# Five two-input operations in place of one strided reduction, for phi's maximum and its sum of weights

## The chip, the cores and the metric

The kernel runs on one core of one Trainium2 chip. The metric is the device time of one execution in microseconds (us), lower is better. The median of the runs of the kernel before is what a change is held against; the profile is of one single execution, whose own time stands beside its span below.

## The reference, cut to what matters

An attention with a small memory feeds two feed-forward blocks. Only the first lines concern the change: `phi` becomes softmax weights `a` over its 32 columns, and `a` gathers keys and values into a memory of 32 rows for each of 4 x 8 heads.

```python
a = phi - np.max(phi, axis=2, keepdims=True)      # phi: 4 x 8 x 576 x 32, the maximum over the 576 tokens
a = np.exp(a)
a = a / (np.sum(a, axis=2, keepdims=True) + 1e-09)
k_m = np.einsum('bhsm,bhsd->bhmd', a, k)
v_m = np.einsum('bhsm,bhsd->bhmd', a, v)
scores = scale * np.matmul(q, k_m.transpose(0, 1, 3, 2))
attn = softmax(scores)                             # over the 32 columns
x = np.matmul(attn, v_m)                           # then as 2304 rows of 512
h = x @ w_in;  g = h / (1 + np.exp(-h));  x = g @ w_out
out = ((x @ w_a) * (x @ w_b)) @ w_out2
```

All arrays come in as 64-bit floats, of which the kernel makes 32-bit values, or pairs of a high and a low part that are multiplied as three products.

## The kernel before, in words

Each batch b goes through `weights(b)`, `memory(b)`, and for its two groups of four heads `turn_q`, `scores` and `softmax`. The feed-forward block starts in between (`unit`: `emit_h` at L279, `emit_y` at L303), as soon as a batch's attention is there, and the second block (`emit_ab`, `emit_out`) follows when all is done.

`weights(b)` is the function that changes. `load_phi` (L416) has put phi of one batch into the tile `ph`: 96 partitions, each with 8 heads x 6 tokens x 32 columns, so a partition holds six tokens of each head. L450 reduces the six tokens on VectorE (DVE) to a maximum per head and column, in `mxa`. Its input is a view with the tokens innermost, so neighbouring elements of the read lie 32 words apart. TensorE transposes `mxa` (L455), L459 reduces over the 96 partitions, and L463 and L465 spread the result back to all partitions. L472 subtracts it, on GpSimd (POOL) for batches 0 to 2 and on DVE for batch 3, and L475 takes the exponential. Batch 0 is done in two halves of four heads (`SPLIT_W`), so L450 runs five times. For batch 3 alone (`SUMS`), L478 reduces the six tokens again, as a sum, and a matmul with a column of ones (L489) finishes it; the other batches get their sums from a matmul with ones in `memory` (L506).

The weights of the feed-forward blocks come in by `load_w` (L93) or, later, `convert` (L157): a transfer into `st`, issued by SyncE (SP), then a run of dependent DVE operations (L107, L110, L113, L117, L124) that builds the 32-bit value, with ScalarE (ACT) and POOL taking a part. `st` has three buffers, so a further load waits until an earlier one has been read for the last time.

The order on each engine is not that of the program text alone. The calls from L593 on give the order in which the work is written down; the tile framework then plans the order of each engine's instructions with its own estimates of what each costs (`schedule_with_timeline_sim=True`, L830), unless a line pins it (`tc.keep_in_program_order`). On the chip each engine runs its list in that fixed order.

Of the kernel before, what the change touches and what calls it, by code (L numbers as in the profile page):

```python
# [14 lines left out]
ALU = mybir.AluOpType  # L15
AX = mybir.AxisListType
# [4 lines left out]
def attn_moe_moe2_kernel(  # L21
# [24 lines left out]
    nc = tc.nc  # L46
# [334 lines left out]
    JP = S // P  # L381
# [8 lines left out]
    def warm_up(w, n):  # L390

        if n:
            jk = ff["y"].tile([128, HALF], F32, tag="yp", name="jk")
            for _ in range(n):
                nc.tensor.matmul(jk[:P, :P], w[:, :P], ones, start=True, stop=True)
# [16 lines left out]
    def heads(b):  # L412

        return [slice(0, 4), slice(4, 8)] if b in SPLIT_W else [slice(0, 8)]
# [17 lines left out]
    def load_q(b, hg):  # L432
# [7 lines left out]
                nc.sync.dma_start(out=qq[r], in_=src[o])  # L440
        st[b]["qq", hg] = qq

    def weights(b, sub=nc.vector):

        e = st[b]["ph"]
        for hs in heads(b):
            nh = hs.stop - hs.start
            n = nh // 4
            mxa = p_s.tile([P, nh, NM], F32, tag="mxa", bufs=2, name="mxa")
            nc.vector.tensor_reduce(  # L450
                out=mxa, in_=e[:, hs].rearrange("p h c m -> p h m c"), op=ALU.max, axis=AX.X
            )
            mxt = ps_t.tile([128, n, P], F32, tag="t", name="mxt")
            for x in range(n):
                nc.tensor.transpose(  # L455
                    mxt[:, x], mxa[:, 4 * x : 4 * x + 4].rearrange("p h m -> p (h m)"), ident[:P, :P]
                )
            mx = p_s.tile([128, n], F32, tag="mx", bufs=2, name="mx")
            nc.vector.tensor_reduce(out=mx, in_=mxt, op=ALU.max, axis=AX.X)  # L459

            dg = p_s.tile([128, n, 128], F32, tag="mxa", bufs=2, name="dg")
            for x in range(n):
                nc.scalar.activation(out=dg[:, x], in_=ident, func=AF.Copy, scale=mx[:, x : x + 1])  # L463
            bc = ps_t.tile([P, nh, NM], F32, tag="t", name="bc")
            nc.tensor.matmul(bc.rearrange("p h m -> p (h m)"), ones, dg.rearrange("p x n -> p (x n)"))  # L465
            if b == 0:
                warm_up(dg[:, 0], WARM[1 + hs.start // 4])
            if sub is nc.gpsimd:
                mxb = p_s.tile([P, nh, NM], F32, tag="mxa", bufs=2, name="mxb")
                nc.scalar.activation(out=mxb, in_=bc, func=AF.Copy)  # L470
                bc = mxb
            sub.tensor_tensor(  # L472
                out=e[:, hs], in0=e[:, hs], in1=bc.unsqueeze(2).to_broadcast([P, nh, JP, NM]), op=ALU.subtract
            )
            nc.scalar.activation(out=e[:, hs], in_=e[:, hs], func=AF.Exp)  # L475
            if b in SUMS:
                es = p_s.tile([P, nh, NM], F32, tag="mxa", bufs=2, name="es")
                nc.vector.tensor_reduce(  # L478
                    out=es, in_=e[:, hs].rearrange("p h c m -> p h m c"), op=ALU.add, axis=AX.X
                )  # L480
                if "sm" not in st[b]:
                    st[b]["sm"] = ps_t.tile([128, 2], F32, tag="t", name="sm")
                for x in range(n):
                    g = hs.start // 4 + x

                    for y in range(2):
                        r = slice(64 * y, 64 * y + 64)
                        hd = 4 * x + (2 * y + 2 * b) % 4
                        nc.tensor.matmul(  # L489
                            st[b]["sm"][r, g : g + 1], es[:, hd : hd + 2].rearrange("p h m -> p (h m)"), ones[:P, :1]  # L490
                        )
# [106 lines left out]
    load_phi(1)  # L598
    load_phi(2)
    weights(0, nc.gpsimd)  # L600
    load_kv(0, 1)
    memory(0)
# [4 lines left out]
    scores(0, 0)  # L607
    load_kv(1, 0)
    weights(1, nc.gpsimd)
    load_wo(0, 0, (nc.vector, nc.vector, nc.vector))  # L610
    turn_q(0, 1)
# [10 lines left out]
    memory(1)  # L622
    load_wo(0, 2, (nc.gpsimd, nc.gpsimd, nc.vector))
    weights(2, nc.gpsimd)
    turn_q(1, 0)
    unit(0, 0, 0, cs=(0, 1))
# [208 lines left out]
```

## Time and profile before

| | us |
|---|---|
| median of 3 runs | 893.93 |
| lowest and highest of them | 891.17, 895.27 |
| the profiled execution, its own time | 895.07 |
| its span, first to last instruction | 893.3 |
| TensorE (PE) busy in the span | 847.2 |
| DVE busy | 536.1 |
| ACT busy | 406.3 |
| POOL busy | 162.5 |

The span lies 1.77 us under the execution's own time. Busy times are sums over the whole span; the first 80 us, in which phi, the keys and the first weights come in, look quite unlike the rest. A row of instruction groups gives line, engine, operation, output and inputs with their shapes, the count, then busy time in us and the mean of one in ns, then the idle time ahead of it. In a timeline a row is start, duration, engine, line.

### The profile page before, as it was taken

How to read it: one execution, taken by the hardware profiler on the slowest of the kernel's cores; microseconds unless marked ns; L12 is line 12 of the kernel's file. 1: busy time of each engine (PE TensorE's matmuls, PEld its weight loads, DVE VectorE, ACT ScalarE, POOL GpSimd, SP SyncE). 2: the span in 40 equal slices, each digit the busy share in tenths (PEclk: the TensorE clock that was granted, in tenths of full speed). 3: DMA queues.
4: the chain of work that ended last, by engine and by line, in shares of the span. 5: the costliest groups of instructions: out<-in, count | busy, mean ns of one | idle time of the engine just before them, and what ended most of it. 6: DMA issues, size and time to landing. Idle time of an engine off the chain costs nothing.

```text
span 893.3 us, 14183 instructions
## 1 busy us (share of the span) xinstructions
PE 847.2 (95%) x5654; PEld 799.8 (90%) x5654; DVE 536.1 (60%) x980; ACT 406.3 (45%) x819; POOL 162.5 (18%) x160
## 2 busy tenths in 40 slices
PE   5458899999999999999999999999999999999998
PEld 4347889999999999999999999999999999999997
DVE  3699688887777677766755544636445552233313
ACT  2347666686566566555444332333333332122211
POOL 3454003422210111121222111111111110000000
PEclk7557999999999999999999999999999999999999
DMA  9998410265752554364764434424343321110012
GB/s 213 244 202 211 108 27 26 83 152 109 156 122 45 116 127 99 85 143 105 160 134 98 92 84 95 95 59 93 85 95 72 83 48 24 36 36 20 24 30 71
DMA packets 49939, 87.16 MB, mean 98 GB/s; under 512 B 4561, under 2 KB 26065, under 8 KB 49873
## 3 DMA queue, kind: packets, MB, share of 16 engines
q1 hardware_dynamic: 33456, 56.50, 24.3%
q0 software_dynamic: 16128, 29.37, 18.7%
q8 instruction: 44, 0.72, 0.3%
q10 hardware_dynamic: 288, 0.39, 0.2%
q14 instruction: 23, 0.18, 0.1%
HBM read 52.17 MB, written 4.72 MB: 64 GB/s over the span
## 4 chain that ended last, share of the span: by engine, by line
PE 80%; DMA 7%; DVE 6%; issue 3%; ACT 2%; SPq 1%; POOL 1%; POOLq 0%; DVEq 0%; ACTq 0%
PE ab L742 32%; PE yp L312 19%; PE op L763 17%; PE hp L288 9%; DMA st<-in_moe_w_in_dram 3%; DMA t_w<-e_w 1%; PE mp L268 1%; PE mp L256 1%; PE sc L556 1%; DMA kv<-in_v_dram 1%; DVE t L113 1%; DMA wo_1l<-t_wo 1%; SPq L427 1%; DVE qT L539 1%; SPq L98 0%
## 5 line engine op out<-in xcount | busy, mean ns | idle before, releaser
L747 DVE TENSOR_TENSOR asb<-ab,asb 128x384 f32<-128x384 f32 x72 | 40.1, 557 | 198.8 <-PE ab L742 196.0
L746 ACT ACTIVATE asb<-ab 128x384 f32<-128x384 f32 x72 | 35.4, 491 | 148.8 <-PE ab L742 148.8
L79 ACT ACTIVATE ph<-asb 128x384 fp32r<-128x384 f32 x72 | 37.6, 522 | 118.9 <-DVE asb L747 118.8
L298 ACT ACTIVATE g<-hp 128x288 f32<-128x288 f32 x128 | 52.3, 411 | 79.9 <-PE hp L288 71.7
L300 DVE TENSOR_TENSOR gl<-g,gh 128x288 fp32r<-128x288 f32 x128 | 62.2, 488 | 38.5 <-ACT gh L299 38.1
L187 POOL DMA_DIRECT2D t_w<-e_w x36 | 31.8, 884 | 145.8 <-DVE e_w L183 130.3
L318 DVE TENSOR_TENSOR y<-yp,y 128x288 f32<-128x288 f32 x104 | 47.3, 456 | 18.4 <-PE yp L312 17.9
L299 ACT ACTIVATE gh<-g 128x288 fp32r<-128x288 f32 x128 | 56.4, 444 | 3.6 <-PE yp L312 0.3
L75 DVE TENSOR_TENSOR pl<-asb,ph 128x384 fp32r<-128x384 f32 x72 | 39.9, 554 | 20.7 <-ACT ph L79 20.7
L79 ACT ACTIVATE yh<-y 128x768 fp32r<-128x768 f32 (+1 forms) x48 | 29.5, 676 | 25.9 <-PE ab L742 25.9
L312 PE MATMUL yp<-gh,wo_1l 128*128 128x288 f32 x128 | 37.8, 296 | 1.5 <-DMA wo_1l<-t_wo 1.5
L312 PE MATMUL yp<-gh,wo_0h 128*128 128x288 f32 x128 | 38.4, 300 | 0.1
L312 PE MATMUL yp<-gh,wo_2h 128*128 128x288 f32 x128 | 38.2, 299 | 0.0
L312 PE MATMUL yp<-gl,wo_3h 128*128 128x288 f32 x128 | 37.8, 297 | 0.0
L312 PE MATMUL yp<-gl,wo_2h 128*128 128x288 f32 x128 | 37.8, 295 | 0.0
L312 PE MATMUL yp<-gl,wo_0h 128*128 128x288 f32 x128 | 37.8, 295 | 0.0
L312 PE MATMUL yp<-gh,wo_2l 128*128 128x288 f32 x128 | 37.7, 295 | 0.0
L312 PE MATMUL yp<-gh,wo_3h 128*128 128x288 f32 x128 | 37.7, 295 | 0.0
L312 PE MATMUL yp<-gl,wo_1h 128*128 128x288 f32 x128 | 37.7, 296 | 0.0
L312 PE MATMUL yp<-gh,wo_1h 128*128 128x288 f32 x128 | 37.7, 294 | 0.0
L312 PE MATMUL yp<-gh,wo_0l 128*128 128x288 f32 x128 | 37.7, 294 | 0.0
L312 PE MATMUL yp<-gh,wo_3l 128*128 128x288 f32 x128 | 37.6, 294 | 0.0
(416 smaller groups left out, 2861.4 us busy)
## 6 DMA issues: line engine op xcount, KB each, us to landing
t_w<-e_w POOLq DMA_DIRECT2D x36, 256.0 KB, 4.9
st_wi<-in_moe_w_in_dram SPq DMA_DIRECT2D x12, 512.0 KB, 4.3
st_wo<-in_moe_w_out_dram SPq DMA_DIRECT2D x12, 512.0 KB, 3.7
st_w<-in_moe_w_a_dram SPq DMA_DIRECT2D x12, 512.0 KB, 3.9
st_w<-in_moe_w_b_dram SPq DMA_DIRECT2D x12, 512.0 KB, 4.0
st_w<-in_moe_w_out_dram SPq DMA_DIRECT2D x12, 512.0 KB, 3.8
kv<-in_k_dram SPq DMA_DIRECT2D x8, 576.0 KB, 11.7
kv<-in_v_dram SPq DMA_DIRECT2D x8, 576.0 KB, 14.3
```

What stands on the lines that cost most here:

```text
L75: eng_lo.tensor_tensor(out=lo, in0=src, in1=hi.bitcast(F32), op=ALU.subtract)
L79: nc.scalar.activation(out=out, in_=in_, func=AF.Copy)
L288: nc.tensor.matmul(hp, a[:, cs], x[b][:, kc, ts], start=(n == 0), stop=(n == 5))
L298: nc.scalar.activation(out=g32, in_=hp, func=AF.Silu)
L299: nc.scalar.activation(out=gh, in_=g32, func=AF.Copy)
L300: nc.vector.tensor_tensor(out=gl, in0=g32, in1=gh.bitcast(F32), op=ALU.subtract)
L312: nc.tensor.matmul(yp, a[:, os], x, start=(n == 0), stop=(n == 3 * len(cs) - 1))
L318: nc.vector.tensor_tensor(out=ys, in0=yp, in1=ys, op=ALU.add)
L742: nc.tensor.matmul(abp, a[:, ks], yy[:, kc], start=(n == 0), stop=(n == 11))
L746: nc.scalar.activation(out=asb, in_=ps[0], func=AF.Copy)
L747: nc.vector.tensor_tensor(out=asb, in0=ps[1], in1=asb, op=ALU.mult)
L763: ins = nc.tensor.matmul(o_t[x], a[:, cols], w, start=(c == 0 and n == 0), stop=(c == 3 and n == 2))
```

## The change

L450 and L478 each become a call of a new helper, `over_tokens`. It makes the result by five two-input operations on DVE: the first takes tokens 0 and 1, each further one takes the result so far and the next token. In each, 32 columns of a head lie side by side in all three operands. The output tile, its shape and everything else stay. The sum's additions keep the order of the tokens.

```diff
+    def over_tokens(out, x, op):
+        for c in range(1, JP):
+            nc.vector.tensor_tensor(out=out, in0=x[:, :, 0] if c == 1 else out, in1=x[:, :, c], op=op)
+
     def weights(b, sub=nc.vector):
...
-            nc.vector.tensor_reduce(
-                out=mxa, in_=e[:, hs].rearrange("p h c m -> p h m c"), op=ALU.max, axis=AX.X
-            )
+            over_tokens(mxa, e[:, hs], ALU.max)
...
-                nc.vector.tensor_reduce(
-                    out=es, in_=e[:, hs].rearrange("p h c m -> p h m c"), op=ALU.add, axis=AX.X
-                )
+                over_tokens(es, e[:, hs], ALU.add)
```

## Rows read from the trace of the kernel before

**Rows 1.** Stretches: length, busy PE, PEld, DVE, ACT, POOL; clock, DMA share, GB/s
```profile
20.00:40.00 20.00, 6.38 (x104) 4.96 (x105) 14.05 (x25) 8.54 (x21) 9.20 (x7) 0.50 1.07 249
40.00:60.00 20.00, 15.13 (x212) 12.02 (x214) 17.48 (x25) 7.17 (x14) 8.12 (x5) 0.59 0.89 195
60.00:80.00 20.00, 12.79 (x51) 8.84 (x44) 19.84 (x33) 11.59 (x27) 14.20 (x8) 0.59 1.08 234
80.00:100.00 20.00, 19.95 (x269) 18.91 (x267) 17.76 (x25) 15.69 (x29) 2.14 (x1) 0.98 0.51 140
```

**Rows 2.** The chain that ended last: start, us, what
```profile
13.05 15.27 DMA st<-in_moe_w_in_dram
...
50.37 2.70 DVE mxa L450
...
78.05 3.63 PE sc L556 x8
...
119.26 2.65 issue
```

**Rows 3.** DVE, groups of instructions by shape, first 130 us
```profile
L113 DVE SCALAR_TENSOR_TENSOR t<-e,t 128x512 uint32<-128x512 uint32 x8 | 9.9, 1232 | 0.2
...
L450 DVE TENSOR_REDUCE mxa<-ph 96x256 f32<-96x1536 f32 x3 | 8.4, 2797 | 1.7 <-DMA ph<-in_phi_dram 1.7
L300 DVE TENSOR_TENSOR gl<-g,gh 128x288 fp32r<-128x288 f32 x16 | 6.9, 447 | 0.6 <-ACT gh L299 0.6
...
L450 DVE TENSOR_REDUCE mxa<-ph 96x128 f32<-96x768 f32 x2 | 2.9, 1471 | 6.5 <-DMA ph<-in_phi_dram 4.5 <-ACT mxb L470 2.0
L478 DVE TENSOR_REDUCE es<-ph 96x256 f32<-96x1536 f32 x1 | 2.9, 2870 | 0.0
...
L127 DVE TENSOR_TENSOR t<-t,e 128x512 f32<-128x512 f32 x4 | 2.7, 663 | 0.0
L75 DVE TENSOR_TENSOR vbd_lo<-vt,vbd_hi 64x64 fp32r<-64x64 f32 x12 | 2.6, 215 | 0.2
...
L472 DVE TENSOR_TENSOR ph<-ph,bc 96x1536 f32<-96x1536 f32 x1 | 1.7, 1740 | 0.0
```

**Rows 4.** DVE in order of time, 9 to 25 us
```profile
9.38 1.38 DVE L539 STREAM_TRANSPOSE qT<-qq 128x1152 f32<-128x1152 f32 x1 [3.43 <-DMA qq<-in_q_dram]
...
12.93 1.47 DVE L450 TENSOR_REDUCE mxa<-ph 96x128 f32<-96x768 f32 x1 [2.03 <-ACT mxb L470]
...
19.85 2.77 DVE L450 TENSOR_REDUCE mxa<-ph 96x256 f32<-96x1536 f32 x1 [1.71 <-DMA ph<-in_phi_dram]
22.55 0.41 DVE L110 TENSOR_SCALAR t<-e 128x512 uint32<-128x512 uint32 x1
22.99 0.69 DVE L113 SCALAR_TENSOR_TENSOR t<-e,t 128x512 uint32<-128x512 uint32 x1
```

**Rows 5.** POOL in order of time, 10 to 92 us
```profile
12.59 1.81 POOL L472 TENSOR_TENSOR ph<-ph,mxb 96x768 f32<-96x768 f32 x1 [7.81 <-ACT mxb L470]
17.92 1.89 POOL L472 TENSOR_TENSOR ph<-ph,mxb 96x768 f32<-96x768 f32 x1 [3.52 <-ACT mxb L470]
...
75.76 3.90 POOL L472 TENSOR_TENSOR ph<-ph,mxb 96x1536 f32<-96x1536 f32 x1
87.88 2.14 POOL L572 TENSOR_TENSOR x<-x,mxq 128x1152 f32<-128x1152 f32 x1 [8.23 <-DVE mxq L571]
```

**Rows 6.** DVE in order of time, 74 to 92 us
```profile
78.29 2.84 DVE L450 TENSOR_REDUCE mxa<-ph 96x256 f32<-96x1536 f32 x1
...
88.25 2.32 DVE L75 TENSOR_TENSOR wo_3l<-t,wo_3h 128x512 fp32r<-128x512 f32 x1
```

**Rows 7.** SP, its queue's issues in order of time, 0 to 90 us
```profile
24.94 0.35 SPq L98 DMA_DIRECT2D st<-in_moe_w_out_dram  x1
```

**Rows 8.** Waits of PE, 0 to 84 us: total, times, longest
```profile
PE kvp L506 <- DMA kv<-in_v_dram: 3.6, 1, 3.6
```

**Rows 9.** Waits of PE, 84 to 140 us: total, times, longest
```profile
PE sm L489 <- DVE es L478: 0.4, 1, 0.4
```

## The prediction

> **What bounds the kernel now.** I read the table of stretches first. From 80 us on PE is full: 19.95 of 20 us in the first stretch after it. Before, three things take turns. Between 20 and 40 us PE has 6.38 us of work and the transfers take 1.07 of the DMA engines' time, so loading is the limit. Between 60 and 80 us DVE is busy 19.84 of 20 us, while PE has 12.79 [rows 1]. The reader should see from this that DVE time is worth something only in a stretch of some 30 us, and after it only where PE happens to wait for a single DVE result.
>
> The chain of waits, read next, says where the changed lines lie in that picture [rows 2]. It runs through a transfer (13.05 to 28.3 us), later through DVE, in which batch 2's maximum stands with 2.70 us, and goes over to PE at 78.05 us. Batch 3's sum stands there too: the 2.65 us called issue, from 119.26 to 121.91, are the time in which L478 ran. PE lost less by it: its waits show 0.4 us for `es` [rows 9], since it had other products until then.
>
> **The price of a step.** The groups by shape give it [rows 3]. A two-input operation of 288 columns takes 447 ns and one of 512 takes 663, so a column costs (663 - 447) / 224 = 0.96 ns, and 256 columns cost 447 - 31 = 416 ns. For 128 columns I go up from the row of 64: 215 + 62 = 277 ns. The steps depend on each other. L110 and L113 do too: L113 starts at 22.99, L110 ended at 22.55 + 0.41 [rows 4], a gap of 0.03 us. So five steps of 256 take 5 x 0.416 + 4 x 0.03 = 2.20 us, five of 128 take 1.50.
>
> The reductions take 2.797, 1.471 and 2.870 us [rows 3]. That is 1.82 ns for each of 1536 elements, while the subtraction of L472, which reads the same tile in runs of 32 words, takes 1740 ns for as many, 1.13 ns each [rows 3]. Here is the gain: the view with tokens innermost reads slowly. Per long maximum it is 2.80 - 2.20 = 0.60 us, for the sum 0.67; a short one loses 0.03. In all DVE is relieved of 3 x 0.60 + 0.67 - 2 x 0.03 = 2.4 us out of 536.
>
> No row shows this very step. Its ends: the columns alone, 256 x 0.96 = 0.25 us, so five in 1.23 and a long maximum better by 1.57; and the row of 512, 0.663, so five in 3.44 and worse by 0.64. I take 0.416, as 288 columns is the nearest row in size, and keep both ends.
>
> The Trainium skill, Vector Engine (DVE) Microarchitecture Reference, section 5.2 (Measured stream behaviour on trn2), puts about 75 ns beside 1.04 ns a column for instructions that follow each other in the queue. By that five steps would be an estimate of 1.71 us and the whole sum about -1.5 us. No row here shows it for operations that wait for each other.
>
> **What comes with two inputs.** DVE's operations of two inputs can be held up by POOL; the reductions are not. Batch 3's maximum ran from 78.29 with POOL busy until 75.76 + 3.90 = 79.66 and took 2.84 [rows 5, 6], 0.04 more than the mean. In contrast `wo_3l`, two inputs of 512 columns, began at 88.25 while POOL worked from 87.88 to 90.02; it took 2.32 and ended 0.55 after POOL did [rows 5, 6]. I read it as: a step that meets a running POOL operation waits for its end.
>
> This is also a rule of the Trainium skill (SBUF — State Buffer, section Who interferes with whom): on this chip `tensor_reduce` never contends with GpSimd, while an instruction with two SBUF inputs waits out a GpSimd instruction that reads SBUF. It speaks against the change. By it the memsets at the start, which read nothing, would hold nobody; no row decides that.
>
> **The six places in turn.**
> - Batch 0, first half (about 4.5 us): nothing. The next DVE work but one, `qT`, sits idle 3.43 us for its transfer [rows 4], which covers 0.03 and more.
> - Batch 0, second half: it starts at 12.93, under POOL's subtraction, 12.59 to 14.40 [rows 4, 5]. Held, it ends at 14.40 + 1.50 = 15.90 instead of 14.40. POOL's second subtraction then starts at 17.92 + 1.50 = 19.42 and ends at 21.31. The products on batch 0's weights come later by as much; PE waited 3.6 us for `v` there [rows 8], which hides it.
> - Batch 1, at 19.85: now under that subtraction, held for 1.46, then 0.60 shorter, so what is behind it on DVE, L110 at 22.55 and its successors, is 0.86 late. They release an `st` buffer, and SP's load of 24.94 waits for that [rows 7], with the other loads behind it in SP's queue. I cost this at nothing, because the DMA engines have 1.07 of their time filled there [rows 1]. Without that cover it is +0.86.
> - Batch 2, at 50.37: on the chain, nothing of POOL named beside it: -0.60.
> - Batch 3's maximum, at 78.29: held 1.37, then 2.20, so it ends 0.73 later. The chain has gone over to PE a quarter of a microsecond before. PE's products from 78.05 to the next DVE operand cover it. Without that cover +0.73.
> - Batch 3's sum: 0.67 less for DVE, of which PE gets the 0.40 that it waited [rows 9]. What is late next is the run of gates and results behind it on DVE, and they move up by the same 0.67.
>
> Sum: -0.60 - 0.40 = -1.0 us. Against the profiled execution, 895.07 (span 893.3), that is 894.1; this execution lies 1.1 above the median of 893.93, so for the median I say 892.9. With the ends it goes from -1.57 - 0.40 = -2.0 to 2 x 0.64 + 0.86 + 0.73 = +2.9.
>
> **What can upset this: the order.** The plan of each engine's order is made anew. That it departs from the text can be seen: `qT` of the call after `memory(0)` runs at 9.38, ahead of batch 0's second maximum at 12.93 [rows 4]. Thirty steps in place of six, with other costs in the plan, can move their neighbours.
>
> **Rivals.** A measurement of this kernel can tell about 0.5%, 4.5 us, from no change.
> - A luckier order. DVE lost much to holding: L113 averages 1.232 us over eight, against 0.69 unheld [rows 3, 4], 4.3 us in all. If the new order lets these fall beside POOL's work, the time is -1.0 - 4.3 = -5.3, 888.6. For it: most of this lies where DVE is the limit. Against it: nothing in the change aims at it, and all eight would have to profit.
> - Steps held in the stretch where DVE is the limit. One instruction becomes five, and between two of them a POOL operation can begin. POOL has 14.20 us in 8 operations between 60 and 80 us [rows 1], 1.8 each. If batch 2's maximum is planned in there, or POOL's work beside it, four holds cost 7.1: 7.1 - 1.0 = +6.1, 900.0. The first hold eats the gain; over 0.5% it takes the fourth. For it: the holding is seen. Against: POOL is busy only 8.12 of 20 us between 40 and 60 [rows 1].
> - The read is no faster in steps: the gain goes, 893.9. L472's row is against it. It is no change, as is my forecast.
>
> **How the numbers follow.** The forecast, with the last rival, gets 0.58: the effect is small by every row, and PE's 800 us behind do not change. The luckier order gets 0.24, the held steps 0.18. The forecast's own range is -2.0 to +2.9 with 2 us of scatter, 890 to 898.8. For 8 in 10 I reach into both others: 886.5 to 899.5. Faster by over 0.5% is 0.24, same 0.58, slower 0.18; the time is the likeliest case's, 892.9.
>
> **What would show it.** Each long maximum as five rows of about 0.42 us, 2.2 from first to last; first steps stretched to about 1.8 us where POOL's subtraction runs; PE's wait for `es` gone; the chain's change to PE near 77.5 us instead of 78.05. It is wrong if the order on DVE between 44 and 78 us is another, if the steps take over 0.55 us, or if PE's start of full work moves by more than 2 us either way.

## The result, and the profile after

The changed kernel takes 904.63 us (median of 4 runs, 899.16 to 908.37) against 894.60 for the kernel before in the same session: ratio 1.0114, 95% interval 1.0068 to 1.016. It is slower by over 0.5%; I had forecast 892.9 and given this side 0.18. The profiled execution of the changed kernel is its quickest, 899.16, with a span of 897.4.

Where the lines of before answer to it: the stretches [rows 1], with the two pieces of 2 us that follow a new pause of PE. Columns as there; the third number from the end is the granted clock.

```profile
20.00:40.00 20.00, 7.22 (x91) 5.24 (x86) 12.23 (x25) 8.20 (x20) 9.64 (x7) 0.50 1.07 254
40.00:60.00 20.00, 10.42 (x218) 8.65 (x216) 18.42 (x34) 7.67 (x13) 7.70 (x6) 0.84 1.00 232
60.00:80.00 20.00, 11.97 (x38) 8.77 (x39) 19.88 (x33) 10.61 (x26) 14.52 (x8) 0.67 0.92 212
80.00:100.00 20.00, 18.65 (x258) 17.49 (x257) 15.79 (x22) 15.52 (x27) 2.13 (x1) 0.97 0.33 99
...
140.00:160.00 20.00, 15.61 (x102) 14.75 (x101) 17.14 (x33) 12.13 (x20) 5.89 (x5) 0.91 0.09 27
...
156.00:158.00 2.00, 2.00 (x12) 2.00 (x11) 2.00 (x5) 0.00 (x0) 0.66 (x2) 0.58 0.71 209
158.00:160.00 2.00, 2.00 (x11) 2.00 (x10) 1.93 (x4) 0.00 (x0) 1.06 (x1) 0.56 0.17 61
```

DVE is as full between 60 and 80 us as it was. PE is idle for 4.4 of the 20 us from 140 us on, where the kernel before had it busy for all 20:

```profile
140.00:160.00 20.00, 20.00 (x148) 19.48 (x147) 15.31 (x30) 15.42 (x30) 7.42 (x6) 1.00 0.09 28
```

The longest of its waits from 84 to 160 us names the place:

```profile
PE yp L312 <- ACT g L298: 4.2, 1, 4.2
```

After this pause PE ran for some 4 us at little over half of its clock (0.58 and 0.56, near 1.2 of 2.4 GHz), then at full clock again.

Batch 2's maximum in DVE's order of time, 48 to 58 us, answers to the single row of 50.37 us [rows 2]:

```profile
48.10 0.41 DVE L446 TENSOR_TENSOR mxa<-ph 96x256 f32<-96x256 f32 x1
48.43 0.74 DVE L572 TENSOR_REDUCE mxq<-x 128x18 f32<-128x576 f32 x1
...
50.61 0.41 DVE L446 TENSOR_TENSOR mxa<-mxa,ph 96x256 f32<-96x256 f32 x1
...
52.28 0.41 DVE L446 TENSOR_TENSOR mxa<-mxa,ph 96x256 f32<-96x256 f32 x1
...
54.04 1.37 DVE L446 TENSOR_TENSOR mxa<-mxa,ph 96x256 f32<-96x256 f32 x1
...
57.59 0.41 DVE L446 TENSOR_TENSOR mxa<-mxa,ph 96x256 f32<-96x256 f32 x1
```

Four of the steps cost what was forecast, 0.41 us, and one, held, 1.37. But the five are not one block: the planner put other work between them, and the maximum takes from 48.10 to 58.00, 9.9 us, in place of 2.7. Compared in the two traces by operation and tile, the order differs in 69 places (runs of instructions) on DVE, 47 on PE, 32 on ACT and 3 on POOL; SP issues its loads in the same order. From 200 us on the two are alike (PE busy for 58.5 and 58.4 of the 60 us to 260, and for 439.5 and 439.1 of the 440 us from 440 on); the loss is made before 200 us.

### The profile page after: what moved, and what is told of

Its sections match the earlier page's. It is cut to its first block, busy times and chain, and to the rows that moved or that the text cites. A ratio compares the mean times of both kernels' runs of the same rounds, so it can differ in the third digit from the quotient of the medians.

```text
span 897.4 us, 14216 instructions
## 1 busy us (share of the span) xinstructions
PE 843.9 (94%) x5654; PEld 798.3 (89%) x5654; DVE 537.6 (60%) x1004; ACT 409.0 (46%) x821; POOL 162.5 (18%) x160
## 4 chain that ended last, share of the span: by engine, by line
PE 77%; DVE 8%; DMA 6%; ACT 4%; issue 3%; SPq 1%; POOL 1%; POOLq 0%; DVEq 0%; ACTq 0%
PE ab L743 32%; PE yp L312 17%; PE op L764 16%; PE hp L288 9%; DMA st<-in_moe_w_in_dram 2%; DMA kv<-in_k_dram 2%; DMA t_w<-e_w 1%; PE mp L268 1%; DVE qT L540 1%; DVE gl L300 1%; PE sc L557 1%; DMA wo_1l<-t_wo 1%; ACT L298 1%; DVE xt L584 1%; SPq L427 0%
## 5 line engine op out<-in xcount | busy, mean ns | idle before, releaser
L300 DVE TENSOR_TENSOR gl<-g,gh 128x288 fp32r<-128x288 f32 x128 | 63.9, 501 | 44.0 <-ACT gh L299 43.6
L75 DVE TENSOR_TENSOR pl<-asb,ph 128x384 fp32r<-128x384 f32 x72 | 40.0, 555 | 21.9 <-ACT ph L79 21.9
```

The source lines that it names most:

```text
L75: eng_lo.tensor_tensor(out=lo, in0=src, in1=hi.bitcast(F32), op=ALU.subtract)
L300: nc.vector.tensor_tensor(out=gl, in0=g32, in1=gh.bitcast(F32), op=ALU.subtract)
```

## The experiments

Each ratio is against the kernel before on the same chip. "Old order" is the order of every engine in the kernel before, "new order" that of the changed kernel. An order is forced by dependencies between neighbours on one engine, which add no semaphore; the names in `order` come from a plan of the one version, and the other version's instructions are put in their places (e1):

```diff
+    for name in order:
+        for n in mine.get(name, ()):
...
+            if e in last:
+                tc.add_manual_dep(
+                    i, last[e], mybir.DependencyInfo(mybir.DependencyClass.NoSync, mybir.DependencyReason.DATA), reason="order"
+                )
+            last[e] = n
```

| run | steps, order | median us | ratio | 95% |
|---|---|---|---|---|
| e1 | five, old | 892.54 | 0.9984 | 0.9956-1.0013 |
| e2 | one reduction, new | 905.61 | 1.0132 | 1.0091-1.0174 |
| e3 | five, new (the changed kernel) | 904.08 | 1.0114 | 1.0063-1.0164 |
| e4 | maxima in five, planned anew | 897.68 | 1.0042 | 1.0014-1.0070 |
| e5 | five, old up to 140 us, then new | 897.79 | 1.0036 | 1.0012-1.0060 |
| e6 | five, new up to 140 us, then old | 901.89 | 1.0086 | 1.0057-1.0115 |
| e7 | five, old up to 105 us, then new | 900.82 | 1.0061 | 1.0033-1.0090 |
| e8 | five in one block, new | 904.77 | 1.0117 | 1.0087-1.0146 |
| e9 | five, new, `g` ahead on ACT | 903.60 | 1.0114 | 1.0079-1.0149 |
| e10 | five, new up to 66 us, then old | 893.30 | 0.9996 | 0.9969-1.0023 |
| e11 | five, new up to 105 us, then old | 898.11 | 1.0054 | 1.0031-1.0077 |
| e12 | sum in five, planned anew | 896.19 | 1.0028 | 1.0003-1.0054 |
| e13 | e11 with `wo_3h` later on ACT | 898.24 | 1.0061 | 1.0038-1.0085 |
| e14 | five, new, `wo_3h` later | 902.56 | 1.0109 | 1.0083-1.0136 |
| e15 | five, new, both moves | 904.43 | 1.0124 | 1.0098-1.0150 |
| e16 | maxima in two halves each | 894.47 | 1.0001 | 0.9972-1.0030 |
| e17 | sum in two halves, planned anew | 894.39 | 0.9993 | 0.9966-1.0020 |
| e18 | e5 with `g` ahead on ACT | 898.24 | 1.0050 | 1.0025-1.0074 |

### The steps without the order, and the order without the steps: e1, e2, e3

e1 takes the old plan and puts five steps in the place of each reduction; e2 takes the new plan and puts the reduction in the place of the last step; e3 is the changed kernel once more.

```diff
 e1
+    for five in (False, True):
+                follow(tc, traced, plain, marks, *plan, 0)
 e2
+    for five in (True, False):
+                follow(tc, traced, plain, marks, *plan, -1)
```

> Every engine runs the list of the kernel before, instruction by instruction; only each of the six reductions is replaced, at its own place, by the five two-input steps without anything between them. Theory A (the new order of the plan costs the time, the steps themselves are worth what was forecast): about 1 us under the kernel before, within -3 to +1 us. Theory B (two-input steps held up by GpSimd cost the time): slow as the changed kernel, +6 to +12 us, and the first steps under GpSimd's subtraction at 13 us and 78 us show 1.4 us more than the 0.41 of the others.

> Every engine runs the list of the changed kernel; only the five steps of each result are taken out and the old single reduction stands at the place of the last of them. No two-input step is left. Theory A (order): slow as the changed kernel, +6 to +12 us over the kernel before. Theory B (held steps): as the kernel before, within 2 us.

> The changed kernel itself, unaltered, for a second profile: the first one was its fastest execution (899.2 us, the others 904 to 908). Theory A: 902 to 908 us with the same order of instructions and the same step lengths; the 4 to 9 us beyond the first profile lie in one or two waits of TensorE in the first 250 us, with a fall of its granted clock behind them. Theory B: the first steps are held longer than in the first profile by as much as the time grows.

Measured: 0.9984, 1.0132 and 1.0114. The order alone costs all of the loss, with reductions too; the steps alone cost nothing and may bring some 1.4 us, which this measurement can't tell from none. So theory A stands and theory B falls. In the traces, PE, ACT and POOL run the same list in e1 as in the kernel before, and in e2 the same as in e3. One detail of theory A failed: e3's profiled execution has a span 4.8 us longer than that of the first profile, and not by one or two later waits. Batch 1's transposes `vt` already start at 68.38 in place of 64.14 us, 4.2 later, with the same order. So executions of one order differ by some us in the first 70 us, and a single trace can't show a difference of that size there.

In e1 the steps can be looked at undisturbed; its DVE groups by shape, first 130 us:

```profile
L446 DVE TENSOR_TENSOR mxa<-mxa,ph 96x256 f32<-96x256 f32 x12 | 5.1, 422 | 0.4
...
L446 DVE TENSOR_TENSOR mxa<-mxa,ph 96x128 f32<-96x128 f32 x8 | 2.3, 288 | 0.3
```

A later step of 256 columns took 0.42 us, one of 128 took 0.29: forecast 0.416 and 0.277. The first step of batch 2 took 0.41 too; those of the places where a hold was forecast are longer. DVE and POOL of e1 in order of time:

```profile
13.26 1.60 DVE L446 TENSOR_TENSOR mxa<-ph 96x128 f32<-96x128 f32 x1 [2.04 <-ACT mxb L473]
14.89 1.25 DVE L446 TENSOR_TENSOR mxa<-mxa,ph 96x128 f32<-96x128 f32 x4
...
20.24 0.95 DVE L446 TENSOR_TENSOR mxa<-ph 96x256 f32<-96x256 f32 x1 [1.01 <-DMA ph<-in_phi_dram]
...
53.82 0.41 DVE L446 TENSOR_TENSOR mxa<-ph 96x256 f32<-96x256 f32 x1
54.27 1.79 DVE L446 TENSOR_TENSOR mxa<-mxa,ph 96x256 f32<-96x256 f32 x4
...
81.15 1.65 DVE L446 TENSOR_TENSOR mxa<-ph 96x256 f32<-96x256 f32 x1
82.83 1.79 DVE L446 TENSOR_TENSOR mxa<-mxa,ph 96x256 f32<-96x256 f32 x4
```

```profile
12.91 1.80 POOL L475 TENSOR_TENSOR ph<-ph,mxb 96x768 f32<-96x768 f32 x1 [8.13 <-ACT mxb L473]
...
78.61 3.90 POOL L475 TENSOR_TENSOR ph<-ph,mxb 96x1536 f32<-96x1536 f32 x1
```

POOL ends at 14.71 and 82.51; the held steps end at 14.86 and 82.80. That is the rule of the Trainium skill (SBUF — State Buffer, section Who interferes with whom) which the prediction cited, and this trace agrees to 0.3 us. In e1's time no cost of it can be told from none, but batch 3's held step stands on the chain of waits that ended last:

```profile
81.15 1.66 DVE mxa L446
...
91.84 2.23 DVE wo_3l L75
...
94.49 0.53 PE yp L312 x2
```

### One half of the change, planned anew: e4, e12

```diff
 e4: only the maxima (shown); e12: only the sum, in the same way
-            nc.vector.tensor_reduce(
-                out=mxa, in_=e[:, hs].rearrange("p h c m -> p h m c"), op=ALU.max, axis=AX.X
-            )
+            over_tokens(mxa, e[:, hs], ALU.max)
```

> Only the maxima are made in five steps, the sum of batch 3 is the old reduction; the order is planned anew. Theory A: the time follows whatever order comes out, anywhere from -3 to +12 us, and it differs from the changed kernel by more than the 0.7 us that the sum's steps save. Theory C (the sum's steps, spread over 6.6 us instead of 2.9, delay batch 3 and starve TensorE at 151 us): back at the kernel before, within 2 us, and no wait of 4 us at 151 us.

> Only the sum is made by five steps, the maxima by the old reduction, and the order is planned anew for that, with nothing forced. The steps themselves are worth -0.4 (PE's wait for es). If every new plan of this kernel costs time about as much as the two seen (+3.8 for the maxima alone, +10.4 for both): 897 to 900. If only a plan with the hole at 151 to 155 us does, and this one has none: 893 to 895. Max alone and sum alone together (+3.8 and this one's) would give the +10.4 only by chance, since each is a plan of its own.

Measured: 1.0042 and 1.0028, both above e1, though e12's interval overlaps e1's. Each is a plan of its own, so the two can't be added, and neither is the whole loss. Theory C had e4 within 2 us of the kernel before; it came out 3.8 us above, with no wait of 4 us at 151 us, but its interval begins at 1.3 us, so this is no clear refutation. e12 had two readings, 897 to 900 and 893 to 895 us; 896.19 lies between them, with a wait of 2.4 us for `g`, and decides neither.

### Where in the kernel the new order costs: e5, e6, e7, e10, e11

A mixed order takes the head of one plan up to the first `hp` product of a batch and the rest from the other plan. The steps are five in all.

```diff
+    cut = lists[0].index(mine[cuts0[2]][0]) + 1   # 2: m2h, about 140 us; 1: m1h, 105 us; 0: m0h, 66 us
+    early = lists[0][:cut]
...
+    for n in early + [n for n in lists[1] if n not in seen]:
```

> Five steps everywhere; every engine runs the order of the kernel before up to the first hp matmul of m2h (138.6 us in the kernel before) and the changed kernel's order from there on. Theory D (5 to 6 us of the loss arise after 140 us, where ACT puts the exponential of x with its table loads ahead of a g and PE starves at 151 to 165 us; the rest, 4 to 6 us, arises before 140 us): about 898, with a PE wait for g of some 4 us near 150 to 160 us. Theory E (all of the loss arises in the stretch that DVE bounds, before 105 us, and the starvation only stands in for a later wait): about 893. Theory F (the sum's five steps, spread out at 119 to 126 us, make it): about 893.

> The reverse: the changed kernel's order up to the first hp matmul of m2h, the order of the kernel before from there on. Theory D: 904.6 - 5.5 = about 899, without the 4 us wait for g near 155 us. Theories E and F: about 904, the whole loss.

> As the first of these, but the change of order comes at the first hp matmul of m1h (105.0 us in the kernel before), so the sum's five steps are spread as in the changed kernel too. Theory D: about 898, no more than with the cut at 140 us. Theory E: about 893. Theory F: over 900, several us above the kernel with the cut at 140 us.

> Five steps; the changed kernel's order up to the first hp matmul of m0h (66 us), the order of the kernel before from there on. Differs from the kernel with the old order in 24 places on DVE, 10 on ACT and 2 on PE. If the loss of the first 105 us is made where DVE loads and splits (before 66 us): about 896. If it is made by hp standing ahead of the next batch's scores on PE (after 66 us): 892 to 893.

> As the kernel with the cut at 66 us, with the cut at the first hp matmul of m1h (105 us). If the parts add up (new order up to 140 us cost +7.5, of which the kernel with the new order from 105 us on lets 3.0 fall to 105 to 140 us): 894.4 + 4.5 = about 898 to 899. If the parts do not add up, because a late start is caught up where PE still waits: 893 to 894.

Measured: 1.0036, 1.0086, 1.0061, 0.9996 and 1.0054. Reckoned from e1 (0.9984), the new order costs 0.12% up to 66 us; 1.0054 - 0.9996 = 0.58% from 66 to 105; 1.0086 - 1.0054 = 0.32% from 105 to 140; and 0.3 to 0.5% after that (1.0114 - 1.0086 from one side, 1.0036 - 0.9984 from the other). The part from 66 to 105 us, about 5 us, is shown: the intervals of e10 and e11 don't overlap. The two later ones are each about as large as what a pair of ratios leaves open. No single place makes the loss, and up to 66 us, which takes in the stretch that loading limits, none can be told from zero. Of the theories E falls with e5 and e7, which it had at 893 us, and F as the whole cause with e5. D gave e5 (897.79 for about 898); e6 and e7 came out 3 us above it, at 901.89 and 900.82, and F's over 900 us for e7 came true, so the order around the sum may have a part too.

### Are the scattered steps to blame: e8

The condition in the edit always holds, so all five steps stand at the place of the first.

```diff
+            if len(was) == 1 or 0 is not None:
+                for a in was:
+                    mine[a] = []
+                mine[was[0]] = new
```

> The changed kernel's order on every engine, but each group of five steps runs without a break at the place of its first step. If the spreading of the steps itself costs the time: 893 to 897, and sm's matmul stands again at about 122 us. If it is the order of the other instructions (theories D and E): 903 to 906, as the changed kernel, since only 17 places on DVE differ.

Measured: 1.0117, no gain. Putting the steps together again does not help once the rest has been planned around them. The traces show what PE does instead, in its transposes `vt` of batches 2 and 3 and the product `sm` between them. First e1, then e3 (the changed kernel in an execution near its median, span 902.2), each in PE's order of time:

```profile
109.35 0.38 PE L527 MATMUL vt<-ident,kvn 128*128 128x128 f32 x2
...
122.77 0.40 PE L490 MATMUL sm<-ones,es 96*64 96x1 f32 x8
...
130.88 0.38 PE L527 MATMUL vt<-ident,kvn 128*128 128x128 f32 x2
```

```profile
112.87 0.38 PE L527 MATMUL vt<-ident,kvn 128*128 128x128 f32 x2
...
131.65 0.40 PE L490 MATMUL sm<-ones,es 96*64 96x1 f32 x8
...
140.07 0.44 PE L527 MATMUL vt<-ident,kvn 128*128 128x128 f32 x2 [1.49 <-ACT kvn L522]
```

From `vt` to `sm` it is 13.4 us in the old order and 18.8 in the new. In e3 the sum's steps run from 123.55 to 130.20 (in the kernel before from 119.26 to 121.91 [rows 2]), so `sm` seems to wait for them. In e8 they are one block; DVE, then PE:

```profile
124.99 0.42 DVE L446 TENSOR_TENSOR es<-ph 96x256 f32<-96x256 f32 x1 [1.54 <-ACT ph L478]
125.45 1.79 DVE L446 TENSOR_TENSOR es<-es,ph 96x256 f32<-96x256 f32 x4
```

```profile
114.32 0.38 PE L527 MATMUL vt<-ident,kvn 128*128 128x128 f32 x2
...
133.09 0.40 PE L490 MATMUL sm<-ones,es 96*64 96x1 f32 x8
...
142.21 0.44 PE L527 MATMUL vt<-ident,kvn 128*128 128x128 f32 x2 [1.85 <-ACT kvn L522]
```

`es` is ready at 127.24, and still `sm` comes at 133.09, again 18.8 us after `vt`: PE's list, that of the changed kernel, has other products ahead of it. From batch 2's `vt` to batch 3's it is 22.2 us in the kernel before and 21.5 in e1, against 27.2 in the changed kernel and in e6, e7 and e9, 27.9 in e8. (From batch 1's to batch 2's it is 43.6 us before, 41.9 in e1 and 44.5 in e3.) That looks like a chain that is 5 us late, but most of the 5 us is work. PE from one `vt` to the next, in e1 and in e3, columns as in [rows 1]:

```profile
109.35:130.88 21.53, 21.16 (x224) 19.52 (x223) 18.49 (x38) 15.05 (x32) 0.34 (x1) 1.00 0.23 50
```

```profile
112.87:140.07 27.20, 25.71 (x260) 24.18 (x259) 19.75 (x39) 18.31 (x35) 2.37 (x2) 1.00 0.18 41
```

The new order does 36 more products there, 4.6 us of PE's time, which the old order does later; only 1.1 us is idle time. And e4, e5 and e11 are slower than the kernel before by 0.36 to 0.54% with 20.7, 21.5 and 21.9 us from `vt` to `vt`. So this lateness by itself is not the loss. What is lost shows in PE's idle time, e1 and then e3:

```profile
0.00:140.00 140.00, 99.19 (x1129) 85.48 (x1130) 103.22 (x186) 71.80 (x152) 46.35 (x36) 0.78 0.72 160
140.00:200.00 60.00, 58.41 (x413) 56.14 (x412) 51.20 (x91) 45.83 (x97) 22.04 (x18) 1.00 0.36 94
```

```profile
0.00:140.00 140.00, 92.84 (x1112) 81.33 (x1112) 99.99 (x179) 71.29 (x144) 44.23 (x36) 0.80 0.71 160
140.00:200.00 60.00, 54.98 (x369) 52.58 (x370) 49.40 (x85) 42.17 (x92) 22.30 (x17) 0.94 0.23 63
```

PE is idle for 40.8 us of the first 140 in e1 and 47.2 in e3, then for 1.6 and 5.0 us up to 200: 9.8 us more in all, where e3's span is 8.9 us longer. From 140 to 200 us it is 5.0 in e5 too, which has the new order there, and 1.6 in e11, which has the old. These are single executions, whose first 70 us scatter by some us, and no run shows which moves of the new order make PE idle.

### Two single holds that looked like the cause: e9, e18, e13, e14, e15

The pause of 4.2 us at `yp` has a plain reason in ACT's list: an exponential of `x` with a table load of 1.28 us on either side, `m3h` and `at_hi` stand ahead of the two `g` that PE needs (ACT of the changed kernel):

```profile
150.14 1.28 ACT L574 ACT_TABLE_LOAD   x1
151.44 0.68 ACT L574 ACTIVATE x<-x 128x576 f32<-128x576 f32 x1
...
153.20 1.28 ACT L298 ACT_TABLE_LOAD   x1
154.49 0.71 ACT L298 ACTIVATE g<-hp 128x288 f32<-128x288 f32 x2
```

e9 puts `g` first in the changed kernel, e18 in e5, where batch 3's `vt` comes as early as in the old order.

```diff
+        moved = act[:153] + act[156:160] + act[153:156] + act[160:]
```

> The changed kernel's order on every engine, with one difference: on ACT the two g and two gh that PE starved for at 151 to 155 us go ahead of the second exponential of x, its m3h and its at_hi, which also saves two table loads of 1.28 us. If this hole is what the order costs after 140 us (kernel with the new order after 140 us only: +3.4): 904.6 - 4 = about 900.5, and no PE wait for g of 4 us. If the exponential that is now later holds PE elsewhere for as long: 904 to 905.

> The kernel with the old order up to 140 us and the changed kernel's order from there on (ratio 1.0036, with the 4.2 us PE wait for g at about 152 to 156 us), with the two g and two gh moved ahead of the second exponential of x on ACT. In the changed kernel this move gave nothing. If that was because the last batch's chain, 5 us late there (kvn transposes 27.2 us apart instead of 21.6), held PE in any case: here, where the chain is on time, the move gives the loss back, 0.998 to 1.001. If the hole is only where PE happens to stand while the order of the 40 us behind it is what costs: 1.002 to 1.005 again.

Measured: 1.0114 and 1.0050, against 1.0114 and 1.0036 without the move. The pause is gone and the time is not. e18's waits of PE, 130 to 260 us, and its stretches:

```profile
PE mp L268 <- DVE m1l L75: 2.0, 1, 2.0
PE yp L312 <- DVE gl L300: 1.1, 2, 0.6
PE hp L288 <- DVE m3l L75: 1.1, 1, 1.1
PE hp L288 <- ACT at_hi L79: 1.0, 1, 1.0
PE yp L312 <- ACT g L298: 0.8, 1, 0.8
...
```

```profile
140.00:160.00 20.00, 17.24 (x118) 15.69 (x117) 14.19 (x27) 12.13 (x22) 4.88 (x4) 1.00 0.10 27
160.00:180.00 20.00, 17.91 (x125) 17.05 (x125) 19.58 (x30) 13.40 (x33) 9.93 (x7) 1.00 0.27 82
```

Between 140 and 180 us five short waits, 4.0 us together (the last four lines), have taken the place of the long one, and PE is idle for 2.8 and 2.1 us in the two stretches; DVE is full in the second, 19.58 of 20 us. The wait of 2.0 us for `m1l` lies behind them, after 180 us; it is 0.5 in e5 and 1.6 in the kernel before. The pause was where the delay showed, not what made it.

The second hold lies in the dearest part: before 90 us ACT stands still for `wo_3h`, with the exponential of phi and a table load behind it. ACT of e11:

```profile
88.12 0.63 ACT L79 ACTIVATE wo_3h<-t 128x512 fp32r<-128x512 f32 x1 [2.57 <-DVE t L127]
```

e13 moves that instruction five places back in e11, e14 in the changed kernel, e15 does both moves there.

```diff
+        moved = act[:64] + act[65:70] + act[64:65] + act[70:]
```

> The kernel whose engines run the changed kernel's order up to 105 us and the old one from there on (ratio 1.0054), with one ACT instruction moved: the last wo_3h, for which ACT stood still for 2.57 us at 85.55 us, goes behind the exponential of phi and the next g and gh (5 places later). If this hold, which keeps the exponential, a table load of 1.28 us and y behind it, is what the new order costs between 66 and 105 us: ratio down by at least half, to 1.001 to 1.003 (894 to 896). If the loss lies in the whole arrangement of DVE's and PE's work and the hold only stands in for it: 1.004 to 1.006.

> The changed kernel's order with the same single move of wo_3h on ACT. By the first reading above: 904.6 - 2.5 to 4 = 900.5 to 902. By the second: 904 to 905.

> The changed kernel's order with both moves on ACT: wo_3h later, and the two g and two gh ahead of the exponential of x (the latter alone gave 1.0114, nothing). By the first reading: 900 to 902, and less than wo_3h's move alone if the starvation at 155 us only counts once the earlier delay is gone (899). By the second: 904 to 905.

Measured: 1.0061, 1.0109 and 1.0124. None comes back toward e1, so the first reading falls. That leaves the second, the arrangement as a whole; it is what remains and was not shown by a run of its own.

### Does any new plan cost it: e16, e17

Both keep the reductions and make them in two halves, e16 the maxima (its plan is that of before but for the added instructions), e17 the sum (38 places on PE, 23 on ACT and 19 on DVE differ).

```diff
 e17
-                nc.vector.tensor_reduce(
-                    out=es, in_=e[:, hs].rearrange("p h c m -> p h m c"), op=ALU.add, axis=AX.X
-                )
+                for z in range(2):
+                    zs, ez = slice(z * nh // 2, (z + 1) * nh // 2), slice(hs.start + z * nh // 2, hs.start + (z + 1) * nh // 2)
+                    nc.vector.tensor_reduce(
+                        out=es[:, zs], in_=e[:, ez].rearrange("p h c m -> p h m c"), op=ALU.add, axis=AX.X
+                    )
```

> The kernel before; each of the five reductions for the maximum is made as two reductions over half of the columns, so five DVE instructions more, about 0.06 us each of fixed cost, 0.3 us in all. The plan of every other engine comes out the same (no place on PE, ACT, POOL and SP differs). Control: ratio 0.998 to 1.002, whichever theory holds.

> The kernel before; only the one reduction for the sum is made as two over half of the columns: one DVE instruction more, under 0.1 us. But the plan comes out anew: 38 places on PE, 23 on ACT and 19 on DVE differ. If any fresh plan of this kernel costs time, whatever the edit (the order as a whole, theory A in its general form): 1.002 to 1.006, as with five steps for the sum alone (1.0028). If the plan only gets worse where the steps are long in all or many: 0.998 to 1.001.

Measured: 1.0001 and 0.9993. A new plan is not dear by itself; e17's is as good as that of before. Its PE is idle for 37.4 us of the first 140 and for 2.9 from there to 200, against 37.7 and 1.6 in the kernel before.

Left open: why the planner, given five steps, orders the rest so much worse. Its estimates stand in no trace. A kernel that beats both was not found; e1, which keeps the old order by force, beats the changed kernel by 1.3% and can't be told from the kernel before.

## Why the prediction was wrong

- **The price of a step: right.** 0.416 and 0.277 us forecast, 0.422 and 0.288 measured in e1, well inside the ends of 0.25 and 0.66. Batch 2's five steps took 2.24 us in e1 (53.82 to 56.06) for a forecast of 2.20.
- **The holds: right in kind and size, their cover in part not.** Batch 0's second half was held for 1.3 us (1.60 against 0.29) and batch 3's first step for 1.2 (1.65 against 0.42); batch 1's, forecast at 1.46, lost 0.5 in e1 (0.95 against 0.42), because the later start left less of POOL's operation. The first shows in PE's waits, 3.1 us for `mxa` in e1 where it was 1.6, in the stretch that loading limits. For batch 3 the prediction had the chain gone over to PE at 78.05, so that 0.73 us more would cost nothing. In e1 the chain runs through the held step and stays on DVE until 94.45 us. In e17, which keeps the reductions for the maximum, it stays there until 89.40, so the 78.05, read from one execution, doesn't hold in others. From the start of batch 3's maximum to the end of `wo_3l` DVE took 12.28 us before [rows 6] and 12.92 in e1, 0.64 more.
- **PE's wait for `es`: gone,** as forecast; e1 lists no wait of `sm`.
- **The sum of -1.0 us: agrees with the change alone, but isn't shown.** e1 gives -1.4 us (0.9984 of 893.91), interval -3.9 to +1.2. With batch 3's 0.64 uncovered the same terms would come to about -0.4, which the interval allows as well.
- **The order: this step failed.** The part on what can upset the forecast named it ("with other costs in the plan, can move their neighbours") and put no term into the sum. That term was the largest: 1.0132 for the order with the old reductions, about +12 us against steps of -1. The rivals took it up on one side only, as the luckier order at -5.3 us. The sign that was to show it did: the order on DVE between 44 and 78 us is another, with batch 2's five steps spread over 9.9 us.
- **The rival of held steps: right side, wrong mechanism.** It gave 900.0. Batch 2's steps ran from 48 to 58 us, outside the stretch of 60 to 80 us, and one of them was held (54.04, 1.37 us) where the rival needed four; e2, which has no steps to be held, is as slow as the changed kernel.
- **The range** ended at 899.5 because it was built from prices of instructions. With a plan made anew it needed a case for an unlucky order as well as a lucky one; a plan moves dozens of places on three engines, and prices of single rows bound none of that.

## What to carry to other kernels

Where a planner makes each engine's order, a change of the number of instructions is two changes: price the instructions from the rows, and give the new order a case of its own on both sides. To part them, run the new instructions in the old order and the old ones in the new. The longest new wait in the trace is not yet the cause; move the one instruction it hangs on, and see whether the time follows. Before a mark in the trace is called late, count the work ahead of it: an order that only does more there first has lost nothing yet, and the idle time of the engine that is the limit tells the two apart.

## What was not expected of the hardware

- Four dependent steps of 256 columns took 1.79 us and four of 128 took 1.25 (e1). Less the last one's own length that is 0.456 and 0.321 from one start to the next: 1.05 ns a column, and 0.19 us beside the columns in each. The Trainium skill (Vector Engine (DVE) Microarchitecture Reference, section 5.2) has about 75 ns there for instructions that follow each other in the queue; for a chain of dependent ones the measurement decides, 0.19. Where an instruction that doesn't need the step follows it, as `mxq` at 48.43 in the changed kernel, it starts 0.33 us after the step did, 0.06 beside the columns, close to the 75 ns of the Trainium skill.
- One pause of PE of 4.2 us was followed by about 4 us near half clock (0.58, 0.56); e18, with the same pause cut into five waits of at most 1.1 us, shows 1.00 in both stretches from 140 to 180 us (0.91 in the next, in which PE waited 2.0 us), and took no less time.
